# A recurrence with sparse attention on one core: scans over every second step, the causal mask inside the maximum, the decay mask on two engines, a first projection in fp32, and a new order

## The chip, the cores and the metric

The kernel runs on one core of a Trainium2 chip. The core has engines that run side by side, each with its own queue of instructions: TensorE (PE, matrix products; PEld is its weight load), VectorE (DVE), ScalarE (ACT), GpSimd (POOL) and SyncE (SP, which here only issues transfers). Semaphores order them. Matrix products write PSUM; everything else lies in SBUF. The metric is the device time of one execution in microseconds. A profile comes from one further execution.

## The reference

The inputs are r, k, v, w of shape (4 batches, 8 heads, 768 steps, 48), a bonus u per head, and the weights of a layer of four attention experts, of which two are taken per token.

```python
for t in range(S):                                   # recurrence
    cur = np.einsum('bhd,bhe->bhde', u[None] * kt, vt)
    y[:, :, t] = np.einsum('bhd,bhde->bhe', rt, state + cur)
    state = wt[:, :, :, None] * state + np.einsum('bhd,bhe->bhde', kt, vt)
...
x = y of all heads side by side                      # (4, 768, 384)
logits = x @ w_gate; topk = the 2 best of 4; w = softmax of their logits
for e in range(E):                                   # 4 experts, 64 wide
    q, k, v = x @ wq[e], x @ wk[e], x @ wv[e]
    scores = np.where(causal, -1000000000.0, scale * (q @ k.transpose(0, 2, 1)))
    a = softmax(scores)
    ye = a @ v @ wo[e]
    out += (w where e was taken) * ye
```

## The kernel before, in words

Work is cut into eight units: batch b, half g of the 768 steps. A unit's 384 steps are six chunks of 64 (C=64, NH=6). Its eight heads go as four pairs p, two heads on the 128 partitions.

The recurrence of a pair. SP loads lt (decay w, k and r, with the 48 features on partitions and steps along columns), nat (v, k, r with steps on partitions) and vy. Two scans on VectorE turn w into running products inside each chunk: `suf` (L407) backwards and `pre` (L411) forwards, each over 390 columns, six chunks of 65; `inv` (L409) is a reciprocal between them. Then k and r are scaled by them, kt (L414) and mr (L416, which overwrites pre). TensorE turns kt (ktp), ScalarE or VectorE brings it to SBUF (kts), ups (L462) is each chunk's contribution to the state, and five steps a pair on VectorE (L471) run the state wst along the chunks. ys (L481) scales the states. Within a chunk, aps (L526) is the 64x64 matrix between steps for two pairs at once; its upper part is kept by a multiplication with dec_mask, am (L535), on VectorE straight out of PSUM: one instruction of 128 partitions for the even pair, two of 64 partitions for the odd one, whose halves lie swapped. yps adds ys times pre (L504) and am times vy (L501) in PSUM. Separately uk (L421), ur (L424), rk (L427) and ux (L434 on ScalarE, six multiplications of 48 columns a pair, or L436 on GpSimd or VectorE) make the bonus term in xn, and addy (L510, one per head) adds yps to it.

The attention of a unit. xn is turned in three thirds of 128 features (xp, L248 or L252). Each is split into xh and xl (L557 ScalarE, L559 VectorE), two parts with fewer bits of mantissa; a product of fp32 accuracy is then three products: high by high, high by low, low by high. So run the projections to q and k (L601: three products to a third, three thirds, for two pairs of experts and for q and k: 36 in a unit) and to v and the gate's logits (L624). Scores (L689) are made for pairs of experts in blocks of 128 rows; four products L694 of a bf16 `causal` with a selection matrix `idh` add -1e9 above the diagonal. VectorE takes the negated maximum out of PSUM (L703), ScalarE the exponential with the row's sum (L705), TensorE turns the result (tp), ScalarE or VectorE copies it (ATa, ATb), and L747 multiplies it with v. Then come the gate's weights, gb (L793) and the output product op (L815).

At the start TensorE runs 94 filler products `warm` (L865) that nothing reads, wherever nothing else is ready.

The order. Every operation is recorded with the engines that may take it, a cost on each, its inputs and its outputs. `order()` then lists the operations engine by engine: each has a due time (its place in its unit's stretch plus a number from the table `WISH`, by kind and unit), and the planner takes the earliest due among those that could start by its own costs (t_dve, t_scan, t_act, t_exp, t_pool and the T_ numbers). It picks the engine where several may take an operation, keeps a `port` between VectorE and GpSimd for the kinds in `BOTH`, and reckons gaps where TensorE changes the shape of its tile. The program is emitted in that order, with a dependency added for the port. One queue of transfers, SP's, carries all loads and stores in the planned order.

Of the kernel before, what the change touches and what calls it, by code (L numbers as in the profile page):

```python
# [19 lines left out]
NP = H // 2  # L20
C = 64
# [5 lines left out]
WB = NH * (C + 1) + 1  # L27
# [7 lines left out]
def t_scan(cols):  # L35
    return 65 + 2.09 * cols
# [6 lines left out]
def t_exp(cols):  # L43
    return 237 + 0.834 * cols


def t_pool(cols):
    return 60 + 2.25 * cols


class Slot:
# [6 lines left out]
    def __call__(self):  # L58
# [14 lines left out]
BOTH = {"DVE": {"suf", "pre", "ys", "kt", "mr", "uk", "ur", "ux", "yl", "wsqk", "wsvg", "wso", "carry", "gate", "masks"},  # L73
        "POOL": {"kt", "mr", "uk", "ur", "ux", "gate", "g4"}}
# [12 lines left out]
class Plan:  # L87
# [8 lines left out]
    def add(self, kind, engs, fn, r=(), w=(), want=None, mode="F", alt=None, claim=()):  # L96

        o = dict(engs=engs, fn=fn, want=(self.now if want is None else want) + WISH[kind][self.unit],  # L100
                 n=len(self.ops), kind=kind, mode=mode, alt=alt, deps=set(), outs=[], slots=[], ready={})
# [21 lines left out]
    def order(self, free, slack=60.0, width=40):  # L123
# [11 lines left out]

        def push(o):
            for e in o["engs"]:
                insort(cand[e], (o["want"], o["n"]))
# [3 lines left out]

        for o in ops:
            if need[o["n"]] == 0:
                push(o)
        done = []
# [3 lines left out]
        while len(done) < len(ops):  # L150
# [52 lines left out]
            for s in o["slots"]:  # L203
                s.left -= 1
                s.ends[e] = max(s.ends.get(e, 0.0), end)
                if s.left == 0:
                    bufs[s.tag][s.idx] = s.ends
            for k in o["outs"]:
                x = ops[k]
                x["ready"][e] = max(x["ready"].get(e, 0.0), end)  # L210
                need[k] -= 1
                if need[k] == 0:
                    push(x)
            done.append(o)
# [5 lines left out]
def rwkv_moe(ctx: ExitStack, tc: tile.TileContext, wkr, vY, nat, uN,  # L220
# [52 lines left out]

    one_suf = cst.tile([128, WB], F32, name="one_suf")
    nc.gpsimd.memset(one_suf, 0.0)
    nc.gpsimd.memset(one_suf[:, 1:WB].rearrange("p (c j) -> p c j", j=C + 1)[:, :, C:C + 1], 1.0)  # L276
    inv_pre = cst.tile([128, NH, C + 1], F32, name="inv_pre")
# [30 lines left out]
    sel = cst.tile([128, 3 * E, HD], BF16, name="sel")  # L308
    tri = cst.tile([128, E, E], F32, name="tri")
# [3 lines left out]
    nc.gpsimd.memset(idh, 0.0)  # L313

    def masks(e):
        nc.scalar.copy(identb, ident)
        for a in range(2):
            for h in range(2):
                p = slice(64 * h, 64 * h + 64)
                nc.scalar.copy(idh[p, a, 64 * a:64 * a + 64], ident[p, 64 * h:64 * h + 64])  # L320

    def masks2(e):
        for a in range(2):
            for h in range(2):
                p = slice(64 * h, 64 * h + 64)
                nc.vector.tensor_scalar(causal[p, a, :], d128[p], 64.0 * (a - h), -1.0e9, op0=ALU.is_gt, op1=ALU.mult)
# [7 lines left out]
    def weights(n, src, cols, parts=1):  # L334
# [4 lines left out]
        wts[n] = (h, l)  # L339
# [11 lines left out]
    def rwkv(b, g, v0, v1):  # L351
# [9 lines left out]

        two = []
        for p in range(NP):
            n = f"{b}{g}{p}"
            want(p / (NP + 1))
            lt = sb([128, WB + 2 * NH * C], F32, "lt", f"lt{n}")
            if first and p == 0:
                load("ld", lambda lt=lt: lt()[:, 0:WB], wkr[b, g, p, :, 0:WB], WB, [(lt, 0)])
                load("ld", lambda lt=lt: lt()[:, WB:], wkr[b, g, p, :, WB:], 2 * NH * C, [(lt, 1)])
            else:  # L370
                load("ld", lt, wkr[b, g, p], WB + 2 * NH * C, [(lt, 0), (lt, 1)])
# [26 lines left out]
            pre = sb([128, NH, C + 1], F32, "pre", f"pre{n}")  # L398
            am = sb([128, NH, C], F32, "am", f"am{n}")

            def sfv(suf=suf):
                return suf()[:, 1:WB].rearrange("p (c j) -> p c j", j=C + 1)

            kt = sb([128, NH, C], F32, "kt", f"kt{n}")


            plan.add("suf", {"DVE": t_scan(WB)}, lambda e, suf=suf, w_=w_: nc.vector.tensor_tensor_scan(  # L407
                rev(suf()), rev(w_()), rev(one_suf), 0.0, op0=ALU.mult, op1=ALU.add), [(lt, 0)], [suf])
            plan.add("inv", {"DVE": 106}, lambda e, sfv=sfv: nc.vector.reciprocal(inv_pre[:, :, 0], sfv()[:, :, 0]),  # L409
                     [suf], ["inv_pre"])  # L410
            plan.add("pre", {"DVE": t_scan(WB)}, lambda e, pre=pre, w_=w_: nc.vector.tensor_tensor_scan(  # L411
                flat(pre()), w_()[:, 0:WB - 1], flat(inv_pre), 0.0, op0=ALU.mult, op1=ALU.add),
                [(lt, 0), "inv_pre"], [pre])
            plan.add("kt", prod(384), lambda e, k_=k_, sfv=sfv, kt=kt: E_[e].tensor_tensor(  # L414
                kt(), k_(), sfv()[:, :, 1:C + 1], op=ALU.mult), [(lt, 1), suf], [kt])
# [614 lines left out]
```

## Time and profile before

| what | value |
|---|---|
| three runs | 363.26, 363.70, 366.65 us, median 363.7 |
| the profiled execution | 363.1 us, its span 361.3 us |
| mean granted clock of TensorE | 0.985 of full speed |
| instructions in the span | 13097 |
| idle of GpSimd before kt, on suf | 35.0 us, 13 times |
| idle of ScalarE before the exponential, on the maximum | 34.3 us, 32 times |
| idle of TensorE's weight load before L504, on ys of GpSimd | 3.9 us, 4 times, longest 1.7 |
| loads by SP | 31 whole lt of 579.5 KB, 32 nat of 432.0 KB, 32 vy of 144.0 KB |

A group's row in the profile names the line, the engine, the operation, output<-input with their shapes and the count; behind the first bar stand the busy time of all and the mean of one in ns, behind the second the engine's idle time just before them and who ended it. Rows of a timeline are start, length, what ran, and in brackets the idle time before. The chain of work that ended last is followed back from the last instruction.

### The profile page before, as it was taken

How to read it: one execution, taken by the hardware profiler on the slowest of the kernel's cores; microseconds unless marked ns; L12 is line 12 of the kernel's file. 1: busy time of each engine (PE TensorE's matmuls, PEld its weight loads, DVE VectorE, ACT ScalarE, POOL GpSimd, SP SyncE). 2: the span in 40 equal slices, each digit the busy share in tenths (PEclk: the TensorE clock that was granted, in tenths of full speed). 3: DMA queues.
4: the chain of work that ended last, by engine and by line, in shares of the span. 5: the costliest groups of instructions: out<-in, count | busy, mean ns of one | idle time of the engine just before them, and what ended most of it. 6: DMA issues, size and time to landing. Idle time of an engine off the chain costs nothing.

```text
span 361.3 us, 13097 instructions
## 1 busy us (share of the span) xinstructions
PE 343.7 (95%) x5357; PEld 267.6 (74%) x5357; DVE 305.0 (84%) x797; ACT 203.2 (56%) x611; POOL 142.0 (39%) x263
## 2 busy tenths in 40 slices
PE   7999989899999999999999999999999999999986
PEld 3555777687876878787877868887787878868755
DVE  6899899779889999988989998998999983567462
ACT  3262354573757645864745646767674464556553
POOL 3466276545462143463853246435333210201010
PEclk9999999789999999999999999999999999999989
DMA  7995547135633634336245344645120000000101
GB/s 251 373 318 184 176 128 256 35 92 174 200 133 116 181 104 135 116 132 201 74 139 187 116 151 133 219 136 161 35 95 24 18 5 33 34 2 3 65 3 65
DMA packets 18060, 45.20 MB, mean 125 GB/s; under 512 B 2000, under 2 KB 9424, under 8 KB 18000
## 3 DMA queue, kind: packets, MB, share of 16 engines
q1 hardware_dynamic: 18000, 44.37, 37.1%
q8 instruction: 42, 0.69, 0.8%
q14 instruction: 18, 0.15, 0.1%
HBM read 39.64 MB, written 4.72 MB: 123 GB/s over the span
## 4 chain that ended last, share of the span: by engine, by line
PE 68%; DVE 16%; ACT 5%; DMA 3%; issue 3%; POOL 3%; SPq 0%; ACTq 0%; DVEq 0%; POOLq 0%
PE pp L601 12%; PE yp L747 9%; PE op L815 7%; PE sp L689 7%; PE tp L248 6%; PE vp L624 5%; ACT a L705 4%; PE tp L252 3%; DVE mx L703 3%; PE warm L865 3%; PE aps L526 3%; PE ups L462 3%; PE yps L504 3%; DVE am L535 2%; DVE wst L471 2%
## 5 line engine op out<-in xcount | busy, mean ns | idle before, releaser
L705 ACT ACTIVATE a<-sp,mx 128x128 f32<-128x128 f32 (+5 forms) x96 | 60.3, 634 | 39.4 <-DVE mx L703 34.3
L703 DVE TENSOR_REDUCE mx<-sp 128x1 f32<-128x128 f32 (+5 forms) x96 | 55.3, 616 | 7.8 <-PE sp L694 5.7
L414 POOL TENSOR_TENSOR kt<-lt,suf 128x384 f32<-128x384 f32 x28 | 26.8, 959 | 46.3 <-DVE suf L407 35.0
L471 DVE SCALAR_TENSOR_TENSOR wst<-wst,suf,ups 112x48 f32<-112x48 f32 x160 | 39.7, 258 | 2.4 <-ACT wst L256 0.2
L434 ACT ACTIVATE xn<-nat,rk 128x48 f32<-128x48 f32 x120 | 30.7, 331 | 15.7 <-DVE rk L427 15.5
L256 ACT COPY ATa<-tp 128x512 f32<-128x512 f32 (+3 forms) x72 | 34.1, 488 | 9.3 <-PE tp L248 6.0
L601 PE MATMUL pp<-xh,wh_qk 128*128 128x384 f32 x96 | 38.5, 401 | 0.0
L421 POOL TENSOR_TENSOR nat<-nat,u_sb 128x288 f32<-128x288 f32 x32 | 25.7, 803 | 31.8 <-DMA nat<-in_nat_dram 21.4
L747 PE MATMUL yp<-ATa,v_sb 128*64 128x384 f32 (+2 forms) x240 | 37.5, 441 | 0.0
L407 DVE TENSOR_TENSOR_SCAN suf<-lt,one_suf 128x390 f32<-128x390 f32 x32 | 31.3, 977 | 2.2 <-DMA lt<-in_wkr_dram 1.3
L248 PE MATMUL tp<-ident,a 128*128 128x128 f32 x191 | 30.2, 282 | 2.8 <-ACT a L705 1.4
L601 PE MATMUL pp<-xl,wh_qk 128*128 128x384 f32 x96 | 32.7, 341 | 0.0
L601 PE MATMUL pp<-xh,wl_qk 128*128 128x384 f32 x96 | 32.7, 340 | 0.0
L411 DVE TENSOR_TENSOR_SCAN pre<-lt,inv_pre 128x390 f32<-128x390 f32 x32 | 31.9, 995 | 0.1
L416 POOL TENSOR_TENSOR pre<-lt,pre 128x384 f32<-128x384 f32 x21 | 19.1, 913 | 28.2 <-DVE pre L411 21.4
L535 DVE TENSOR_TENSOR am<-aps,dec_mask 64x384 f32<-64x384 f32 (+1 forms) x48 | 26.6, 554 | 3.6 <-PE aps L526 2.8
L248 PEld LDWEIGHTS tp<-ident,a 128*128 128x128 f32 x191 | 22.2, 142 | 8.3 <-ACT a L705 4.9
L504 PE MATMUL yps<-ys,pre 64*64 64x48 f32 (+1 forms) x704 | 25.1, 222 | 2.1 <-POOL ys L481 2.0
L689 PE MATMUL sp<-Kh,Qh 64*128 64x384 f32 (+4 forms) x128 | 26.6, 396 | 0.4 <-DVE am L535 0.3
L865 PE MATMUL warm<-one_suf 128*128 128x512 bf16 x94 | 25.5, 410 | 1.4 <-POOL one_suf L276 1.4
L504 PEld LDWEIGHTS yps<-ys,pre 64*64 64x64 f32 (+1 forms) x704 | 21.3, 134 | 7.3 <-POOL ys L481 3.9
L501 PE MATMUL yps<-vy,am 64*64 64x48 f32 x768 | 25.9, 219 | 0.2 <-issue 0.2
(134 smaller groups left out, 876.9 us busy)
## 6 DMA issues: line engine op xcount, KB each, us to landing
lt<-in_wkr_dram SPq DMA_DIRECT2D x31, 579.5 KB, 4.7
nat<-in_nat_dram SPq DMA_DIRECT2D x32, 432.0 KB, 4.1
vy<-in_vY_dram SPq DMA_DIRECT2D x32, 144.0 KB, 2.7
out_dram<-ob SPq DMA_DIRECT2D x24, 192.0 KB, 1.9
w_qk<-in_wqk_dram SPq DMA_DIRECT2D x1, 768.0 KB, 7.8
w_vg<-in_wvg_dram SPq DMA_DIRECT2D x1, 390.0 KB, 7.3
lt<-in_wkr_dram SPq DMA_DIRECT2D x1, 384.0 KB, 5.0
w_o<-in_wo_dram SPq DMA_DIRECT2D x1, 384.0 KB, 4.0
```

The lines of the kernel that those rows point to most:

```text
L248: nc.tensor.transpose(o()[:, i * 128:i * 128 + 128], src, ident)
L256: nc.scalar.copy(o, i)
L411: plan.add("pre", {"DVE": t_scan(WB)}, lambda e, pre=pre, w_=w_: nc.vector.tensor_tensor_scan(flat(pre()), w_()[:, 0:WB - 1], flat(inv_pre ...
L471: nc.vector.scalar_tensor_tensor(new, ws[0:112, c0 + c - 1, :], sfv()[0:112, c, 0:1], u()[0:112, o], op0=ALU.mult, op1=ALU.add)
L504: nc.tensor.matmul(yps[h]()[half(q), o], pre()[r, c, 0:C], ys()[r, c, :], start=i == 0, stop=False)
L535: nc.vector.tensor_tensor(am()[o], aps()[i, 0:NH * C].rearrange("p (c j) -> p c j", j=C), dec_mask[i, None, :].to_broadcast([i.stop - i.st ...
L601: nc.tensor.matmul(pp()[:, 0:384], w[:, qk, k, cs], x()[:, k, :], start=(k == j == 0), stop=(k == j == 2))
L689: nc.tensor.matmul(spv(x)[:, h, :], q()[p, t], flat(k())[p, o], start=j == 0, stop=j == 2 and h < np_ - 1)
L703: plan.add("max", {"DVE": t_dve(n)}, lambda e, x=x, mx=mx: nc.vector.tensor_reduce(mx(), spv(x), axis=AX.XY, op=ALU.max, negate=True), [sp ...
L705: plan.add("exp", {"ACT": t_exp(n)}, lambda e, x=x, y=y, mx=mx, a=a: nc.scalar.activation(a()[:, 0:n].rearrange("p (a n) -> p a n", a=np_) ...
L747: nc.tensor.matmul(yp()[e * 64:e * 64 + 64, lo:hi], v_sb[ep]()[:, j, e * 64:e * 64 + 64], at, start=(j == 0), stop=(j == nj - 1))
L865: plan.add("warm", {"PE": 216}, lambda e: nc.tensor.matmul(w()[:, 0:512], wz[:, 0:128], wz, start=True, stop=True), [], [w], want=1e6 if i ...
```

## The change

Six things are changed, and every number of the order with them.

1. Scans over every second step. The host lays out w, k and r with even and odd steps apart. w2 (L428) is the product of two neighbouring steps' decays; the scans suf (L430) and pre (L434) run over w2, 198 columns each. k of the even steps is multiplied by the odd step's decay (kw, L437) and r of the odd steps by the even step's (rw, L439), both in place, 192 columns each. kt (L441) and mr (L443) take 384 columns as before, with the scan's value used for two neighbouring steps and an output in which the two are interleaved again. lt grows from 1159 to 1166 columns.
2. The causal mask inside the maximum. The products L694 and idh are gone. `causal` is one row of zeros with a triangle of -1e9 at its end, in SBUF; a `tensor_tensor_reduce` on VectorE (L752) adds it to the scores, negates, writes the result to SBUF (tile a) and takes the minimum. It compiles to two instructions, the second of which brings out the accumulated minimum. The exponential (L757) then works in place on a, with scale -1.
3. The decay mask. An am is either masked on VectorE out of PSUM (L558, as before), or copied by ScalarE (L564) and then masked in place by GpSimd (L558 on POOL); the planner chooses, and where VectorE took it the second operation is dropped (`skip`).
4. One ux and one addy per pair instead of one per head.
5. The first unit's x is not split: xh stays fp32, there is no xl, and its projections (L639, L670) are plain fp32 products with the unsplit weights, each third by itself as soon as it is there.
6. The planner: costs of exponential, GpSimd and scores, a table ONLY that fixes an engine for some kinds and units, a new WISH table. The order of loads at the start is different too: two vy loads stand ahead of the first lt.

```diff
@@ order: an operation that was taken over is skipped
+            if o["skip"] is not None and o["skip"]["e"] == "DVE":
+                o["e"], o["t"], o["end"] = None, 0.0, 0.0
+                finish(o, o["ready"])
+                return
@@ scans
-            plan.add("suf", {"DVE": t_scan(WB)}, lambda e, suf=suf, w_=w_: nc.vector.tensor_tensor_scan(
-                rev(suf()), rev(w_()), rev(one_suf), 0.0, op0=ALU.mult, op1=ALU.add), [(lt, 0)], [suf])
+            plan.add("w2", prod(WB), lambda e, w2=w2, w_=w_: E_[e].tensor_tensor(w2(), w_(0), w_(1), op=ALU.mult),
+                     [(lt, 0)], [w2])
+            plan.add("suf", {"DVE": t_scan(WB)}, lambda e, suf=suf, w2=w2: nc.vector.tensor_tensor_scan(
+                rev(suf()), rev(w2()), rev(one_suf), 0.0, op0=ALU.mult, op1=ALU.add), [w2], [suf])
...
+            plan.add("kw", prod(192), lambda e, k_=k_, wv=wv: E_[e].tensor_tensor(
+                k_()[:, 0], k_()[:, 0], wv(1), op=ALU.mult), [(lt, 0), (lt, 1)], [(lt, 2)])
...
+            plan.add("kt", spread(384), lambda e, k_=k_, sfv=sfv, kt=kt: E_[e].tensor_tensor(
+                mixed(kt), k_(), both(sfv()[:, :, 1:]), op=ALU.mult), [(lt, 1), (lt, 2), suf], [kt])
@@ decay mask
-                    plan.add("am", {"DVE": 575 if x == 0 else 565}, mask, [(apk, x)], [(am, h)])
+                def masked(e, src, dst, o=slice(0, 128)):
+                    E_[e].tensor_tensor(dst, src, dec_mask[o, None, :].to_broadcast([o.stop - o.start, NH, C]), op=ALU.mult)
+
+                def evict(e, x=x, am=am, aps=apss[x]):
+                    for o, i in ((half(0), half(1)), (half(1), half(0))) if x else ((slice(0, 128),) * 2,):
+                        src = aps()[i, 0:NH * C]
+                        if e == "ACT":
+                            nc.scalar.copy(flat(am()[o]), src)
+                        else:
+                            masked(e, src.rearrange("p (c j) -> p c j", j=C), am()[o], o)
+                o = plan.add("am", {"ACT": 495 if x == 0 else 880, "DVE": 470 if x == 0 else 1090}, evict, [(apk, x), "dmask"], [am])
+                plan.add("msk", {"POOL": t_pool(384)}, lambda e, am=am: masked(e, am(), am()), [am], [am], skip=o)
@@ first projection
+                if first:
+                    wf = wts["qk"][2]
+
+                    def mm(e, k=k):
+                        nc.tensor.matmul(pp()[:, 0:384], wf()[:, (qk * 3 + k) * 256:(qk * 3 + k) * 256 + 256][:, cs], xh()[:, k, :],
+                                         start=k == 0, stop=k == 2)
+                    plan.add("proj", {"PE": 645}, mm, [(xh, k), wf] + ([pk] if k else []), [pk], claim=(K if qk else Q)[ep])
+                    continue
@@ scores, maximum and exponential
-                for a in range(2):
-                    for x in range(2):
-                        p = slice(64 * x, 64 * x + 64)
-                        nc.tensor.matmul(spv(x)[:, np_ - 1, w - 128:w], idh[p, a, :], causal[p, a, :], start=False, stop=a == 1)
...
-                plan.add("max", {"DVE": t_dve(n)}, lambda e, x=x, mx=mx: nc.vector.tensor_reduce(
-                    mx(), spv(x), axis=AX.XY, op=ALU.max, negate=True), [sp], [mx])
+                def lowest(e, x=x, mx=mx, a=a):
+                    nc.vector.tensor_tensor_reduce(
+                        out=a()[:, 0:n].rearrange("p (a n) -> p a n", a=np_), in0=spv(x),
+                        in1=causal[:, S - n:S].rearrange("p (a n) -> p a n", a=np_), scale=-1.0, scalar=3.0e38,
+                        op0=ALU.add, op1=ALU.min, accum_out=mx())
+                plan.add("max", {"DVE": t_dve(n) + T_TTR}, lowest, [sp, "masks"], [mx, a])
...
-                    a()[:, 0:n].rearrange("p (a n) -> p a n", a=np_), spv(x), AF.Exp, bias=mx(),
-                    accum_out=asum()[:, i, y:y + 1]), [sp, mx], [a, (asum, i, y)])
+                    a()[:, 0:n], a()[:, 0:n], AF.Exp, bias=mx(), scale=-1.0,
+                    accum_out=asum()[:, i, y:y + 1]), [mx, a], [a, (asum, i, y)])
@@ numbers of the order (one row of each table)
+ONLY = dict(
+    am="00000100",
...
-    addy=[-237.86, -225.24, -20.82, -95.05, -242.81, -38.73, -115.81, -23.26],
+    addy=[-144.26, -153.99, 0.61, 39.08, 79.54, 3.02, -136.24, -149.46],
...
-T_SC = (492, 561, 733, 902, 1084, 1261)
+T_SC = (385, 454, 626, 795, 977, 1154)
+T_TTR = 12
```

What the order does, in three places. A name is a tile and the numbers behind it unit and pair (suf001: batch 0, half 0, pair 1), then a running number. First VectorE at the start, before:

```order
L407 SCALAR_TENSOR_TENSOR suf000_131<-lt000_108,one_suf_66 128x390
L409 RECIPROCAL inv_pre_69<-suf000_131 128x6
L411 SCALAR_TENSOR_TENSOR pre000_147<-lt000_108,inv_pre_69 128x390
L407 SCALAR_TENSOR_TENSOR suf001_156<-lt001_116,one_suf_66 128x390
L416 TENSOR_TENSOR pre000_147<-lt000_108,pre000_147 128x6x64
L409 RECIPROCAL inv_pre_69<-suf001_156 128x6
L414 TENSOR_TENSOR kt001_174<-lt001_116,suf001_156 128x384
```

and now:

```order
L430 SCALAR_TENSOR_TENSOR suf000_132<-w2000_127,one_suf_68 128x198
L437 TENSOR_TENSOR lt000_110<-lt000_110 128x192
L439 TENSOR_TENSOR lt000_110<-lt000_110 128x192
L432 RECIPROCAL inv_pre_71<-suf000_132 128x6
L441 TENSOR_TENSOR kt000_145<-lt000_110,suf000_132 128x2x192
L434 SCALAR_TENSOR_TENSOR p2000_149<-w2000_127,inv_pre_71 128x198
L443 TENSOR_TENSOR pre000_156<-lt000_110,p2000_149 128x2x192
L428 TENSOR_TENSOR w2001_164<-lt001_120 128x199
```

The first pair's kt, which GpSimd took before, is now VectorE's, while GpSimd makes its w2.

Second TensorE where unit 0's projection begins, before (the rows ahead are fillers):

```order
L865 MATMUL warm_126<-one_suf_66 128x512
L601 MATMUL pp0000_676<-xh00_431,wh_qk_101 128x384
L601 MATMUL pp0000_676<-xh00_431,wl_qk_102 128x384
L601 MATMUL pp0000_676<-xl00_442,wh_qk_101 128x384
L601 MATMUL pp0000_676<-xh00_431,wh_qk_101 128x384
```

and now, at the last third:

```order
L918 MATMUL warm_122<-causal_66 128x512
L261 MATMUL xp002_662<-ident_77,xn00_265 128x128 x3
L639 MATMUL pp00_466<-xh00_455,w_qk_253 128x384 x4
L261 MATMUL ktp010_692<-ident_77,kt010_647 128x128 x3
L639 MATMUL pp0010_478<-xh00_455,w_qk_253 128x384 x2
```

Four of the twelve products stand earlier, among the fillers behind xp000, and two more a few rows on.

Third the masks and maxima of VectorE in unit 1, before:

```order
L535 TENSOR_TENSOR am010_891<-aps010_854,dec_mask_86 128x384
L535 TENSOR_TENSOR am011_899<-aps010_854,dec_mask_86 64x384 x2
L409 RECIPROCAL inv_pre_69<-suf013_879 128x6
L703 TENSOR_REDUCE mx0011_932<-sp00010_739 128x1
L510 TENSOR_TENSOR xn01_594<-yps010_901,xn01_594 128x3x48 x2
```

and now:

```order
L558 TENSOR_TENSOR am011_808<-aps010_774,dec_mask_95 64x384 x2
L682 COPY lg00_818<-vp000_767 128x4
L499 SCALAR_TENSOR_TENSOR wst1_83<-wst1_83,suf011_681,ups011_751 112x48 x3
L752 ISA a0000_835,mx0000_836<-sp00000_820,causal_66 128x128
L752 ISA mx0000_836 128x1
```

Only the odd pair's am is still there; each maximum has become two rows, the first with a second output.

More of the change, by code (lines that the diff above doesn't have):

```diff
@@ L94, in __init__, with add @@
         self.unit = 0
-    def add(self, kind, engs, fn, r=(), w=(), want=None, mode="F", alt=None, claim=()):
+    def add(self, kind, engs, fn, r=(), w=(), want=None, mode="F", alt=None, claim=(), skip=None):
+        only = ONLY.get(kind, "0" * 8)[self.unit]
+        if only != "0" and len(engs) > 1:
+            engs = {e: t for e, t in engs.items() if (e == "DVE") == (only == "2")}
         o = dict(engs=engs, fn=fn, want=(self.now if want is None else want) + WISH[kind][self.unit],
-                 n=len(self.ops), kind=kind, mode=mode, alt=alt, deps=set(), outs=[], slots=[], ready={})
+                 n=len(self.ops), kind=kind, mode=mode, alt=alt, deps=set(), outs=[], slots=[], ready={}, skip=skip)
         for k in r:
@@ L202, in order @@
             o["t"], o["e"], o["end"] = t, e, end
[L203 to L214, printed above, removed]
+            finish(o, {e: end})
         self.span = max(o["end"] for o in ops)
@@ L311, in rwkv_moe, with masks3 @@
                    allow_small_or_imprecise_dtypes=True)
[L313 removed]
     def masks(e):
         nc.scalar.copy(identb, ident)
[L317 to L320 removed]
+    def masks3(e):
+        nc.vector.tensor_scalar(dec_mask[0:64], d128[0:64, 0:C], 0.0, None, op0=ALU.is_gt)
+        nc.vector.tensor_scalar(dec_mask[64:128], d128[64:128, 0:C], -64.0, None, op0=ALU.is_gt)
     def masks2(e):
[L323 to L326, printed above, removed]
+        nc.vector.tensor_scalar(causal[:, S - 128:S], d128, 0.0, -1.0e9, op0=ALU.is_gt, op1=ALU.mult)
         nc.vector.tensor_scalar(onehot, dcol, drow, None, op0=ALU.is_equal)
@@ L542, in rwkv @@
         want(NP / (NP + 1))
-        xh = sb([128, 3, 384], F32R, "xh", f"xh{b}{g}")
-        xl = sb([128, 3, 384], F32R, "xl", f"xl{b}{g}")
-        allx = [(xn, p, h) for p in range(NP) for h in range(2)]
+        xh = sb([128, 3, 384], F32 if first else F32R, "xh", f"xh{b}{g}")
+        xl = xh if first else sb([128, 3, 384], F32R, "xl", f"xl{b}{g}")
         need = {0: [0, 1], 1: [1, 2], 2: [2, 3]}
@@ L620, in vproj, with mm @@
                 step(0.333)
+                if first:
+                    wf = wts["vg"][2]
+                    def mm(e, k=k):
+                        nc.tensor.matmul(vp()[:, 0:260], xh()[:, k, o], wf()[:, k * 260:k * 260 + 260], start=k == 0, stop=k == 2)
+                    plan.add("vproj", {"PE": 440}, mm, [(xh, kk) for kk in range(3)] + [wf] + ([vp] if k else []), [vp], claim=v_sb)
+                    continue
                 def mm(e, k=k):
```

319 lines of the change are left out of this document (186 added, 133 removed).

## The prediction

> **What bounds the kernel now.** I read the busy times first, then the same by stretch, then the chain of work that ended last, then the groups.
>
> ```profile
> span 361.3 us, 13097 instructions
> PE 343.7 (95%) x5357; PEld 267.6 (74%) x5357; DVE 305.0 (84%) x797; ACT 203.2 (56%) x611; POOL 142.0 (39%) x263
> 0.00:39.30 39.30, 35.07 (x506) 18.49 (x507) 33.16 (x86) 15.06 (x43) 19.97 (x35) 1.00 0.80 284
> 39.30:280.00 240.70, 232.82 (x3875) 188.25 (x3874) 221.45 (x578) 145.09 (x449) 112.26 (x189) 0.99 0.42 133
> 280.00:361.30 81.30, 75.83 (x980) 60.88 (x978) 50.38 (x135) 43.07 (x121) 9.73 (x39) 0.98 0.07 25
> PE 68%; DVE 16%; ACT 5%; DMA 3%; issue 3%; POOL 3%; SPq 0%; ACTq 0%; DVEq 0%; POOLq 0%
> ```
>
> A window's row gives its ends and length, the busy time of PE, PEld, DVE, ACT and POOL, then clock, DMA share and GB/s. The cuts are mine: 39.3 us is the start of unit 0's projection, and at 280 us the scans are over. Up to 39.3 PE mostly runs fillers and the loads and VectorE set the pace. From 39.3 to 280 TensorE is 97% busy (232.8 of 240.7) and VectorE 92% (221.5): two engines at the limit, and the chain is PE's with DVE pieces in it. After 280 PE is 93% busy and VectorE 62%. So a microsecond taken from VectorE alone in the middle stage is worth less than a microsecond, and the same holds for TensorE.
>
> **VectorE, part by part.**
>
> ```profile
> L411 DVE TENSOR_TENSOR_SCAN pre<-lt,inv_pre 128x390 f32<-128x390 f32 x32 | 31.9, 995 | 0.1
> L407 DVE TENSOR_TENSOR_SCAN suf<-lt,one_suf 128x390 f32<-128x390 f32 x32 | 31.3, 977 | 2.2 <-DMA lt<-in_wkr_dram 1.3 <-POOL ys L481 0.9
> L535 DVE TENSOR_TENSOR am<-aps,dec_mask 64x384 f32<-64x384 f32 x32 | 17.8, 555 | 0.7
> L510 DVE TENSOR_TENSOR xn<-yps,xn 128x144 f32<-128x144 f32 x64 | 16.4, 297 | 2.4 <-PE yps L501 2.1
> L613 DVE TENSOR_TENSOR Kl<-pp,Kh 128x384 fp32r<-128x384 f32 x16 | 8.8, 550 | 1.7 <-ACT Kh L612 1.6
> L703 DVE TENSOR_REDUCE mx<-sp 128x1 f32<-128x384 f32 x16 | 8.3, 551 | 2.9 <-PE sp L694 1.9 <-ACT a L705 0.8
> L630 DVE COPY lg<-vp 128x4 f32<-128x4 f32 x24 | 3.7, 154 | 2.2 <-ACT v_sb L256 1.9 <-PE vp L624 0.2
> 9.37 0.53 DVE L416 TENSOR_TENSOR pre<-lt,pre 128x384 f32<-128x384 f32 x1
> 9.82 0.18 DVE L409 RECIPROCAL inv_pre<-suf 128x6 f32<-128x6 f32 x1
> 9.92 0.51 DVE L414 TENSOR_TENSOR kt<-lt,suf 128x384 f32<-128x384 f32 x1
> ```
>
> (The last three rows are a timeline: start, length.) A row counts about 0.08 us that the next one overlaps: the 0.53 at 9.37 is followed at 9.82, the 0.18 at 9.82 at 9.92. I count a row less 0.08. Between 144 columns (297 ns) and 384 (550) one column costs 1.05 ns and the rest 0.145 us, which is 0.065 after the overlap. A scan of 390 columns at 0.98 us then costs 2.1 ns a column, and one of 198 about 0.56: 0.42 less. Then:
> - 64 scans: -26 us (64 x 0.42, rounded down). That half the columns do not give half the time by more than the fixed 0.145 is my assumption. Ends -24 and -27.
> - New products: w2 on VectorE 18 times at 199 columns, kw and rw 33 times at 192, each 0.27: +13.8.
> - Decay masks: 48 become 29, 19 x 0.47: -8.9. They move to ScalarE and GpSimd (below).
> - Additions L510: 64 of 144 columns become 32 of 288: -64 x 0.22 + 32 x 0.37 = -2.2.
> - Work that changes engine in the new order: kt and mr +10 at 0.47, uk and the in-place r product +13 at 0.37, kts +7 at 0.47; ys -5, ux -6, ob -4, xl -3, v_sb -4 and small ones. Together +12.8 - 9 = +3.8, at the same price by columns.
> - The maxima. A masked maximum reads the scores from PSUM and the mask from SBUF, adds, writes 128 to 768 columns and reduces. No row shows that. The nearest: a reduction of 384 columns from PSUM takes 551 ns and a two-input subtraction of 384 columns with one input in PSUM 550, so one column a beat for either. I take no change. Upper end: 2.1 ns a column as the scan has, since both combine two operations (rival 4). Lower end: the same.
> - The second instruction of each maximum, which brings out the accumulated value: 96 of them. Nearest row: the 128x4 copy, 154 ns, less 0.08 = 0.07: +6.7. Ends 0 and 200 ns less 0.08 (ScalarE's accumulator read, quoted below), +11.5.
>
> Sum on VectorE: -26 + 13.8 - 8.9 - 2.2 + 3.8 + 6.7 = -12.8, ends -20 and -6. In the middle stage it is about -10: seven of eight units' scans and masks, and 70 of the 96 readings.
>
> [...]
>
> **TensorE.**
>
> ```profile
> 39.30:280.00 240.70, 10.58 (x140) 4.39 (x140) 0.99 0.42 133
> 280.00:361.30 81.30, 3.85 (x52) 1.62 (x52) 0.98 0.07 25
> 296.05 0.29 PE L694 MATMUL sp<-causal,idh 64*128 64x128 bf16 x4
> 296.17 0.35 PE L252 MATMUL xp<-ident,xn 64*128 64x64 f32 x6
> 39.34 3.14 PE pp L601 x18
> 190.34 1.51 PE L747 MATMUL yp<-ATa,v_sb 128*64 128x384 f32 x8
> 191.68 0.82 PE L747 MATMUL yp<-ATb,v_sb 128*64 128x256 f32 x8
> ```
>
> The first two rows are the windows of L694 alone: 140 and 52 mask products, four to a block of scores. Their rows overlap, so a block costs from its start to the next work's: 0.12 us (296.05 to 296.17). 35 blocks in the middle stage: -4.2; 13 after: -1.6. Unit 0's projection: 18 products in 3.14 us (a row of the chain) is 0.52 for the three that make a third. The fp32 product that takes their place: eight 64-column records in 1.34 us (190.34 to 191.68) are two pairs, 0.67 a pair that fills 128 columns, so 12 x (0.67 - 0.52) = +1.8; if a pair's halves ran one after another, a third would be 0.34 and the change -2.2. Four of the twelve now run before xp002 in place of fillers: -4 x 0.67 = -2.7. The nine of v: +0.5 by the same ratio. Middle stage: -4.2 + 1.8 - 2.7 + 0.5 = -4.6. The fillers keep their count (94) and take only idle time.
>
> **ScalarE and GpSimd.**
>
> ```profile
> L705 ACT ACTIVATE a<-sp,mx 128x128 f32<-128x128 f32 (+5 forms) x96 | 60.3, 634 | 39.4 <-DVE mx L703 34.3 <-PE ktp L252 1.6 <-DVE inv_pre L409 1.6
> L705 ACT ACTIVATION_READ_ACCUMULATOR a<-sp,mx 128x1 f32 x96 | 19.2, 200 | 0.0
> L434 ACT ACTIVATE xn<-nat,rk 128x48 f32<-128x48 f32 x120 | 30.7, 331 | 15.7 <-DVE rk L427 15.5
> L414 POOL TENSOR_TENSOR kt<-lt,suf 128x384 f32<-128x384 f32 x28 | 26.8, 959 | 46.3 <-DVE suf L407 35.0 <-DVE pre L411 3.4 <-DVE wl_vg L345 2.9
> L803 ACT CAST yh<-yr 128x384 fp32r<-128x384 f32 x14 | 7.1, 518 | 7.6 <-DVE yr L801 7.6
> L612 ACT CAST Kh<-pp 128x384 fp32r<-128x384 f32 x16 | 7.7, 483 | 3.1 <-PE pp L601 2.7
> ```
>
> The exponentials read SBUF instead of PSUM: a cast of 384 columns takes 518 ns from SBUF and 483 from PSUM, 96 x 0.035 = +3.4. 19 mask copies at 0.4 (483 less 0.08): +7.6. 30 more L434 multiplications at 0.25: +7.5. ScalarE is 60% busy in the middle stage and waits 34.3 us for maxima, so I cost this at nothing; what hides it is that waiting. GpSimd loses about a third of kt (959 ns a piece), uk and ur and gains 13 kw, 18 rw, 14 w2 (0.5 each by columns) and 17 masks (0.96): about +22 to 164, 45% of the span; in the middle stage 112 becomes about 130 of 240. It stays off the bound by itself; as a step in chains it is rival 1.
>
> Behind ScalarE's new mask copies wait exponentials and score evictions, and behind GpSimd's masks the next pair's products; the second product L501 waits for the mask.
>
> **The start.**
>
> ```profile
> 5.71 0.97 DVE L407 TENSOR_TENSOR_SCAN suf<-lt,one_suf 128x390 f32<-128x390 f32 x1 [1.29 <-DMA lt<-in_wkr_dram]
> 7.01 1.57 DVE L411 TENSOR_TENSOR_SCAN pre<-lt,inv_pre 128x390 f32<-128x390 f32 x1
> 6.81 0.95 POOL L414 TENSOR_TENSOR kt<-lt,suf 128x384 f32<-128x384 f32 x1 [4.12 <-DVE suf L407]
> 1.17 2.38 SPq L265 DMA_DIRECT2D lt<-in_wkr_dram  x5
> ```
>
> SP issues five loads in 2.38 us, 0.48 each; the new order puts two vy loads ahead of the first lt: +1.0 before the first scan, and w2 on GpSimd another 0.7. Against it the shorter scans and no xl (-0.6). The rows of VectorE up to unit 0's last addition count 87 instead of 83, about +1.3 us by columns. PE has 31 fewer fillers to run through, so the first projection can come when its thirds are ready. I take 0 (ends -2 and +3).
>
> **The half clock.**
>
> ```profile
> 60.00:80.00 20.00, 17.97 (x241) 14.48 (x241) 15.80 (x45) 12.54 (x45) 10.95 (x18) 0.83 0.28 88
> 64.33 2.25 POOL ys L481
> 66.63 0.33 PE L504 MATMUL yps<-ys,pre 64*64 64x48 f32 x8 [1.51 <-POOL ys L481]
> ```
>
> Here TensorE waits 1.5 us for a ys on GpSimd, and the granted clock in these 20 us is 0.83: 3.4 us of clock are lost. A new order has other waits. Ends 0 and -4.9 (wait and clock gone); I take -2, since the shorter scans let ys be made earlier but GpSimd is fuller.
>
> **The sum.** Start 0. Middle stage: -4.6 if TensorE alone set it, about -10/0.92 = -11 if VectorE alone did; I take -7.5, between them, because both are over 90%. Half clock -2. Last stage: -1.6 for masks, and up to +1.3 where a maximum and its reading stand on the path (0.11 a block): -0.8. Together -10.3: span 351.0. The execution profiled was 363.1 beside its span of 361.3, +1.8, and the median of the runs, 363.7, is 0.6 above it: 353.4, said as 353.5.
>
> **Rivals.**
> 1. The decay mask becomes the wait (slower). The mask was one DVE row of 0.55 us; on 17 occasions it is now a copy (0.48), a hand-over and a GpSimd product (0.96 by the kt row), about 1.2 us later, on two engines whose queues hold other work. If each held L501 and PE found nothing else, +20 us in place of -10: span +10, 373. It decides when half of the 17 are exposed. For it: the scan at 7.01 took 1.57 instead of 0.97 while GpSimd ran kt at 6.81, so the two engines block each other, and GpSimd's work grows by 22 us. Against: a mask may wait behind other units' matmuls, as PE has a second unit's attention to run. Chance 0.13. [...]
> 2. TensorE holds and the start slips: -4.6 - 0.8, +2.7 at the start, no gain in the half clock: about 361 for a run, within 1%. For it: the 97%. Chance 0.20.
> 3. VectorE was what held PE: -11 and the whole half-clock gain, -5, -1: 347. For it: 92% busy with PE fed by it. Chance 0.12.
> 4. The masked maximum runs at the scan's 2.1 ns a column. 448 columns on average x 1.05 x 96 = +45 on VectorE: near 395. Against: the 551 beside 550. Chance 0.03.
>
> **How the numbers follow.** The forecast itself, 349 to 358, has 0.5; with 0.02 for what I have not thought of. Within 1% is 360.0 to 367.3, about what a measurement of this kernel can tell from no change. Faster: 0.5 + 0.12 + a quarter of rival 2 and 0.01 = 0.68. Same: the rest of rival 2 and partly exposed masks, 0.18. Slower: rivals 1 and 4 less those, 0.14. The range reaches to rival 3 and to rival 2: 345 to 362.
>
> **What would show it.** Scan rows near 0.56 us and DVE busy near 292; two rows to each maximum, the first at about 0.55 for 384 columns; GpSimd near 164; no mask products on PE; PEclk full in the slices at 60 to 80 us; unit 0's projection at 38 to 42 us; PE's waits for ys and am. It would be wrong if PE's idle before L501 or L504 grows by several us, if DVE's time falls by less than 6, or if PE's busy time falls without the span.

## The result and the profile after

The changed kernel takes 353.64 us (median of four runs, 351.11 to 354.13) against 364.64 for the kernel before beside it (363.26 to 366.65): ratio 0.968, 95% interval 0.961 to 0.975. A second set gave 353.58 against 362.9, 0.973 (0.966 to 0.981). The profiled execution took 351.11 us with a span of 349.2. The forecast, 353.5, hit the median; the sum behind it, 351.0 for the span, was 1.8 us too high for this execution and 3 too low for that of the second set (354.0). Some executions of a kernel lie more than 1.5% above its fastest; the ratios leave these out, the medians don't.

The page of the changed kernel, as far as it answers to the lines shown of before:

```profile
span 349.2 us, 12872 instructions
PE 331.4 (95%) x5139; PEld 257.3 (74%) x5148; DVE 294.9 (84%) x909; ACT 217.9 (62%) x648; POOL 158.5 (45%) x294
PE 60%; DVE 23%; DMA 5%; ACT 4%; issue 3%; POOL 3%; SPq 0%; ACTq 0%; POOLq 0%; DVEq 0%
```

TensorE's busy time fell by 12.3 us and the span by 12.1: its idle time is what it was. Not all of the 12.3 us are instructions: the granted clock was 0.985 in the profile of before and is 0.999 here, which over 361.3 us is about 5 us of slower work (an estimate). VectorE's fell by 10.1, ScalarE's rose by 14.7 and GpSimd's by 16.5. Now the same by stretch. The borders are drawn anew: in this order the projection of unit 0's last third starts at 40.45 us, and the scans are over at 289 instead of 280.

```profile
0.00:40.60 40.60, 34.75 (x477) 18.37 (x486) 32.19 (x93) 14.86 (x43) 16.22 (x32) 1.00 0.76 265
40.60:289.00 248.40, 240.18 (x3965) 192.02 (x3968) 229.92 (x717) 165.79 (x503) 133.19 (x229) 1.00 0.41 131
289.00:349.20 60.20, 56.43 (x713) 46.88 (x704) 32.76 (x103) 37.26 (x103) 9.14 (x34) 0.99 0.10 34
```

The middle stretch is 7.7 us longer and the last one 21 us shorter: the new order does more attention while the scans still run. So the terms by stage can't be checked one against one, only their sum. In the middle TensorE is 97% and VectorE 93% busy, as before.

The groups that the change touched:

```profile
L434 DVE TENSOR_TENSOR_SCAN p<-w,inv_pre 128x198 f32<-128x198 f32 x32 | 21.4, 668 | 0.2
L430 DVE TENSOR_TENSOR_SCAN suf<-w,one_suf 128x198 f32<-128x198 f32 x32 | 19.4, 619 | 4.3 <-POOL w L428 2.4 <-POOL ys L509 1.9
L428 DVE TENSOR_TENSOR w<-lt 128x199 f32<-128x199 f32 x18 | 7.0, 394 | 0.0
L437 DVE TENSOR_TENSOR lt<-lt 128x192 f32<-128x192 f32 x19 | 7.0, 374 | 1.6 <-DMA lt<-in_wkr_dram 1.6
L439 DVE TENSOR_TENSOR lt<-lt 128x192 f32<-128x192 f32 x14 | 4.9, 350 | 0.6 <-DMA lt<-in_wkr_dram 0.6
L752 DVE CUSTOM_DVE_ANT_0 a<-sp,causal 128x384 f32<-128x384 f32 x16 | 8.5, 547 | 0.2 <-PE sp L741 0.2
L752 DVE DVE_READ_ACCUMULATOR2_ANT mx<- 128x1 f32 x96 | 7.9, 83 | 0.0
L757 ACT ACTIVATE a<-a,mx 128x128 f32<-128x128 f32 (+5 forms) x96 | 63.9, 667 | 19.6 <-DVE mx L752 18.0
L558 POOL TENSOR_TENSOR am<-am,dec_mask 128x384 f32<-128x384 f32 x17 | 17.1, 1005 | 9.5 <-ACT am L564 7.1 <-DVE Kl L658 1.0 <-DVE suf L430 0.8
```

The scans' mean is 619 and 668 ns. The masked maximum of 384 columns takes 547 ns where the reduction took 551. Its second instruction has a row of 83 ns. A timeline shows what that costs:

```profile
111.26 0.68 DVE L752 CUSTOM_DVE_ANT_0 a<-sp,causal 128x512 f32<-128x512 f32 x1
111.86 0.08 DVE L752 DVE_READ_ACCUMULATOR2_ANT mx<- 128x1 f32 x1
111.86 0.69 DVE L752 CUSTOM_DVE_ANT_0 a<-sp,causal 128x512 f32<-128x512 f32 x1
```

The next instruction starts in the same moment as the reading: it costs the queue nothing. So it is after 84 of the 96 readings; behind most of the others VectorE waits for another engine.

### The profile page after: what moved, and what is told of

Its sections match the earlier page's. It is cut to its first block, busy times and chain, and to the rows that moved or that the text cites. A ratio compares the mean times of both kernels' runs of the same rounds, so it can differ in the third digit from the quotient of the medians.

```text
span 349.2 us, 12872 instructions
## 1 busy us (share of the span) xinstructions
PE 331.4 (95%) x5139; PEld 257.3 (74%) x5148; DVE 294.9 (84%) x909; ACT 217.9 (62%) x648; POOL 158.5 (45%) x294
## 4 chain that ended last, share of the span: by engine, by line
PE 60%; DVE 23%; DMA 5%; ACT 4%; issue 3%; POOL 3%; SPq 0%; ACTq 0%; POOLq 0%; DVEq 0%
PE pp L646 10%; PE sp L741 8%; PE yp L799 7%; PE op L867 6%; PE vp L676 6%; PE tp L261 5%; DVE wst L499 3%; DVE am L558 3%; PE tp L265 3%; DMA lt<-in_wkr_dram 3%; DMA nat<-in_nat_dram 3%; DVE a L752 2%; PE yps L532 2%; PE ups L490 2%; PE aps L553 2%
## 5 line engine op out<-in xcount | busy, mean ns | idle before, releaser
L757 ACT ACTIVATE a<-a,mx 128x128 f32<-128x128 f32 (+5 forms) x96 | 63.9, 667 | 19.6 <-DVE mx L752 18.0
L752 DVE CUSTOM_DVE_ANT_0 a<-sp,causal 128x128 f32<-128x128 f32 (+5 forms) x96 | 56.6, 617 | 8.3 <-PE sp L741 7.7
L461 ACT ACTIVATE xn<-nat,rk 128x48 f32<-128x48 f32 x150 | 36.5, 324 | 14.1 <-DVE rk L454 13.9
L646 PE MATMUL pp<-xh,wh_qk 128*128 128x384 f32 x84 | 32.2, 383 | 0.0
L443 POOL TENSOR_TENSOR pre<-lt,p 128x384 f32<-128x384 f32 x20 | 18.7, 937 | 21.2 <-DVE p L434 15.4
L918 PE MATMUL warm<-causal 128*128 128x512 bf16 x85 | 23.9, 418 | 2.4 <-POOL causal L288 1.4
L509 POOL TENSOR_TENSOR ys<-wst,suf 112x288 f32<-112x288 f32 (+1 forms) x25 | 17.8, 714 | 15.4 <-DVE wst L499 13.0
L441 POOL TENSOR_TENSOR kt<-lt,suf 128x384 f32<-128x384 f32 x19 | 17.7, 937 | 15.2 <-DVE suf L430 7.7
L799 PEld LDWEIGHTS yp<-ATa,v_sb 128*64 128x64 f32 x240 | 15.3, 136 | 12.5 <-issue 9.1
L430 DVE TENSOR_TENSOR_SCAN suf<-w,one_suf 128x198 f32<-128x198 f32 x32 | 19.4, 619 | 4.3 <-POOL w L428 2.4
```

Of the source, the lines that this page charges most:

```text
L461: nc.scalar.mul(xn()[:, i, (2 * p + h) * D:(2 * p + h + 1) * D], vn()[:, i, h * D:(h + 1) * D], rk()[:, i, h:h + 1])
L646: nc.tensor.matmul(pp()[:, 0:384], w[:, qk, k, cs], x()[:, k, :], start=(k == j == 0), stop=(k == j == 2))
L752: nc.vector.tensor_tensor_reduce(out=a()[:, 0:n].rearrange("p (a n) -> p a n", a=np_), in0=spv(x), in1=causal[:, S - n:S].rearrange("p (a ...
L757: plan.add("exp", {"ACT": t_exp(n)}, lambda e, x=x, y=y, mx=mx, a=a: nc.scalar.activation(a()[:, 0:n], a()[:, 0:n], AF.Exp, bias=mx(), sca ...
L799: nc.tensor.matmul(yp()[e * 64:e * 64 + 64, lo:hi], v_sb[ep]()[:, j, e * 64:e * 64 + 64], at, start=(j == 0), stop=(j == nj - 1))
L918: plan.add("warm", {"PE": 216}, lambda e: nc.tensor.matmul(w()[:, 0:512], wz[:, 0:128], wz, start=True, stop=True), [], [w], want=1e6 if i ...
```

## The experiments

All kernels below keep the order of the kernel that they start from, unless it says otherwise: only what is emitted in a place is altered, not what the planner is told. Medians are given with the ratio to the kernel before in the same set and its 95% interval. Where a time is given as + or -, a run of the changed kernel is compared with 353.58, the median of the run that comes first here, and a run of the kernel before with the median of that kernel in its own set.

**The changed kernel again.** No edit.

> The changed kernel itself once more, as the base for the runs beside it: 351 to 354 us, ratio to the kernel before 0.965 to 0.972, granted clock over 0.99.

353.58 us, ratio 0.973 (0.966 to 0.981). Missed in part: the ratio lies just above what was expected, one of the four runs, the profiled one, took 355.77 us, and two of the four had a granted clock of 0.988 and 0.990. More on the clock below.

**The causal products' time given back to TensorE.**

```diff
...
+                for a in range(2):
+                    for x in range(2):
+                        p = slice(64 * x, 64 * x + 64)
+                        nc.tensor.matmul(spv(x)[:, np_ - 1, w - 128:w], causal[p, 0:128], causal[p, 0:128], start=False, stop=a == 1)
```

> The changed kernel with four bf16 products of zeros added to each block of scores, in the place where the causal products stood; the order is otherwise the same. Theory A (TensorE sets the pace from 40 us on): 48 blocks x 0.12 us = +5.8 us over the changed kernel, 359 us. Theory B (VectorE sets it, TensorE has slack): under +2 us, 355 us or less. Both halves bound: about +3.5.

358.68 us, +5.1; ratio 0.985 (0.976 to 0.993). The two profiles at full clock (1.000 here, 0.999 in the first of the changed kernel) differ by 353.4 - 349.2 = 4.2 us. Theory A's 5.8 came out at 70 to 90%.

**VectorE's saving given back.**

```diff
+            def more(w2=w2):
+                nc.vector.tensor_tensor_scan(junk, w2()[:, 0:MORE], one_suf[:, 0:MORE], 0.0, op0=ALU.mult, op1=ALU.add)
...
+            def scan1(e, suf=suf, w2=w2, more=more):
+                more()
...
+MORE = 46
```

> The changed kernel with a scan of 46 columns into an unread tile ahead of each of the 64 scans, 0.16 us each, +10 us on VectorE, which is all that VectorE's busy time had fallen (305.0 to 294.9); the order is the same. Theory A (TensorE): under +3 us, under 356.5. Theory B (VectorE): +8 to +11 us, 362 to 364.

357.6 us, +4.0; ratio 0.981 (0.972 to 0.989). VectorE's busy time rose by 12.5 us (307.4), more than the 10 that were meant. So neither theory: some third of VectorE's time shows. The intervals of this run and of the one above overlap that of the changed kernel, so each alone is worth less than the pair that follows.

**Both given back.**

> The changed kernel with both costs given back at once: four products of zeros to each block of scores (+5.1 us alone) and the 46-column scan ahead of each scan (+4.0 alone). If the two engines hold the time one after another, in different places: +9, 362 to 364, which is the time before, and the parts explain the whole gain in this order. If they hide one another: +5 to +6, 359, and some 4 us of the gain are the order's own.

361.67 us against 363.26 for the kernel before, ratio 0.995 (0.992 to 0.998): 2.2 to 2.7 of the 2.7 to 3.2% are gone. At the same clock all of it is: the four runs at a granted clock of 0.994 or 0.995 that the ratio counts have a median of 362.5 us, where the kernel before has 361.5 at that clock (below). The profile at full clock:

```profile
span 358.0 us, 13327 instructions
PE 339.8 (95%) x5340; PEld 261.7 (73%) x5340; DVE 305.9 (85%) x973; ACT 218.3 (61%) x648; POOL 157.6 (44%) x294
```

The span is 358.0 against 349.2, +8.8, with both engines' busy times close to those of before (343.7 and 305.0). The costs add up (4.2 or 5.1, and 4.0), as they would if the two engines held the time in different places, one after the other. It isn't ruled out that part of this is only the disturbance of a fitted order, which knows nothing of the work that was put in. So these costs are rather upper bounds of what the parts are worth.

**The decay masks back on VectorE.**

```diff
-                        if e == "ACT":
-                            nc.scalar.copy(flat(am()[o]), src)
-                        else:
+                        if True:
                             masked(e, src.rearrange("p (c j) -> p c j", j=C), am()[o], o)
...
-                plan.add("msk", {"POOL": t_pool(384)}, lambda e, am=am: masked(e, am(), am()), [am], [am], skip=o)
+                plan.add("msk", {"POOL": t_pool(384)}, lambda e: None, [am], [am], skip=o)
...
+        if o["kind"] == "am":
+            o["e"] = o["how"] = "DVE"
...
+        if o["kind"] == "msk":
+            continue
```

> The changed kernel with all decay masks on VectorE straight out of PSUM, at the place of ScalarE's copies, without the 17 products on GpSimd; nothing else moves. VectorE +9 us, ScalarE -8, GpSimd -16. Theory A (TensorE): within 2 us of the changed kernel. Theory B (VectorE): +5 to +9 us. If the way over ScalarE and GpSimd had been what TensorE waits for: -2 us or more.

357.39 us, +3.8; ratio 0.983 (0.976 to 0.990), between theories A and B, part of it clock (0.986 to 0.993 in its four runs). VectorE's busy time rose by 8.3 us to 303.2. The way over ScalarE and GpSimd is not what holds the kernel: without it the kernel is slower, not faster, and in the changed kernel's profile TensorE's products waited for a mask of GpSimd once, for 0.2 us, and its weight loads twice, for 0.6 us in all.

**The same savings in the order of before.** First without the causal products:

```diff
-                for a in range(2):
-                    for x in range(2):
-                        p = slice(64 * x, 64 * x + 64)
-                        nc.tensor.matmul(spv(x)[:, np_ - 1, w - 128:w], idh[p, a, :], causal[p, a, :], start=False, stop=a == 1)
```

> The kernel before without the 192 causal products (the causal mask is left out of the result), in the same order. Theory A (TensorE sets the pace): 48 x 0.12 = -5.8 us, 358 to 359 us. Theory B (VectorE): under -2 us.

363.81 us against 362.74, ratio 1.003 (1.000 to 1.007): nothing, outside theory A's range, where giving the same products back to the changed kernel cost 4 to 5 us. The middle stretch of this kernel:

```profile
39.30:280.00 240.70, 227.69 (x3727) 182.72 (x3726) 220.34 (x576) 144.58 (x448) 112.39 (x189) 0.99 0.43 133
```

TensorE's busy time there fell from 232.8 to 227.7 us, and in the same time the other engines got through as much as before (576 instructions on VectorE instead of 578, 448 on ScalarE instead of 449, 189 on GpSimd in both): the five microseconds are idle now. Some 1 to 2 of them are clock and not products (an estimate): at a granted clock of 0.83 at 60 to 80 us the kernel before lost 3.4 us, and this profile lost 1.2 to 2.3 in the stretch, by the 0.99 in the row above and the 0.994 over its span of 359.7 us. One place, in the timelines of TensorE, VectorE and GpSimd; the first two rows are of the kernel before, the others of this one:

```profile
104.47 0.40 PE L252 MATMUL xp<-ident,xn 64*128 64x64 f32 x6 [0.82 <-DVE xn L510]
103.44 0.45 DVE L427 TENSOR_REDUCE rk<-nat 128x6 f32<-128x288 f32 x1 [0.85 <-POOL nat L424]
103.86 0.40 PE L252 MATMUL xp<-ident,xn 64*128 64x64 f32 x6 [1.84 <-DVE xn L510]
102.84 0.45 DVE L427 TENSOR_REDUCE rk<-nat 128x6 f32<-128x288 f32 x1 [2.00 <-POOL nat L424]
103.21 0.51 DVE L510 TENSOR_TENSOR xn<-yps,xn 128x144 f32<-128x144 f32 x2
99.62 0.80 POOL L421 TENSOR_TENSOR nat<-nat,u_sb 128x288 f32<-128x288 f32 x1 [1.44 <-DMA nat<-in_nat_dram]
101.26 0.79 POOL L421 TENSOR_TENSOR nat<-nat,u_sb 128x288 f32<-128x288 f32 x1 [0.84 <-PE yps L504]
```

TensorE comes to xp earlier and waits 1.84 us (0.82 before) for L510, which stands in VectorE's queue behind an rk that waits 2.00 us (0.85 before) for a product of GpSimd; GpSimd had itself stood waiting shortly before, for a load (1.44 us) and for a yps of TensorE (0.84 us). Neither TensorE nor VectorE was short of time here: the next thing in the queue wasn't ready.

**Then with additions in place of the scans, and with both.**

```diff
-            ... nc.vector.tensor_tensor_scan(rev(suf()), rev(w_()), rev(one_suf), 0.0, op0=ALU.mult, op1=ALU.add)
+            ... nc.vector.tensor_tensor(suf(), w_(), one_suf, op=ALU.add)
...
-            ... nc.vector.tensor_tensor_scan(flat(pre()), w_()[:, 0:WB - 1], flat(inv_pre), 0.0, op0=ALU.mult, op1=ALU.add)
+            ... nc.vector.tensor_tensor(flat(pre()), w_()[:, 0:WB - 1], flat(inv_pre), op=ALU.add)
```

> The kernel before with each of the 64 scans of 390 columns replaced by one addition of 390 columns (the recurrence's products of decays are left out of the result), in the same order: 0.40 us less each, -26 us on VectorE. Theory A (TensorE): -3 us or less. Theory B (VectorE): -15 us or more. Both bound together: -5 to -9.

358.94 us, ratio 0.990 (0.984 to 0.995): -3.8 us for 23 us less on VectorE (busy 281.6 instead of 305.0), between theory A's -3 and the -5 to -9 of both bound together. Part of it is clock: the two runs at 0.994 or 0.995 have a median of 358.9 against 361.5 for the kernel before at that clock.

> The two together: no causal products and additions in place of the scans (both left out of the result), in the order of before. Theory A: about -6 to -9 us, 355 to 358. Theory B: -15 to -18. If each had only hidden the other, more than the sum of the two alone.

360.9 us, ratio 0.993 (0.988 to 0.997), by the medians no better than the additions alone; no range that was expected was met. Nine of its ten runs had a granted clock of 0.976 to 0.986; the one at 0.995 took 357.12. Theory B is out, and in this order what was taken off TensorE (5.8 us as counted) and VectorE (23) is worth 3 to 4 us together at the same clock: the five runs at 0.985 or 0.986 have a median of 360.4 against 363.4, the one at 0.995 has 357.1 against 361.5.

**A new order from the old due times.**

```diff
-T_SC = (492, 561, 733, 902, 1084, 1261)
+T_SC = (385, 454, 626, 795, 977, 1154)
...
-            plan.add("suf", {"DVE": t_scan(WB)}, ...
+            plan.add("suf", {"DVE": t_dve(WB)}, ...
```

(and the same for pre; otherwise as with both)

> The kernel before without the causal products and with additions in place of the scans (both left out of the result), as in the run with both, but with these costs told to the planner, which makes a new order by the old due times. If the old order is what kept the saving (in-order queues that wait for what was planned there): 350 to 356 us. If due times have to be fitted anew to the costs: 358 or more, as without replanning (360.9).

372.92 us, ratio 1.028 (1.023 to 1.032): 12 us slower than the same work in the old order. The second expectation had the direction, but named 360.9 for it.

```profile
span 370.9 us, 12759 instructions
PE 340.0 (92%) x5191; PEld 262.1 (71%) x5191; DVE 292.5 (79%) x819; ACT 201.0 (54%) x596; POOL 124.3 (33%) x252
```

Every engine has less to do than in the kernel before, and TensorE's share fell from 95% to 92%. Here an order worked out from due times that belong to other costs is worse than a stale one.

**The half clock.** Fillers in the wait that had come before it:

```diff
+                    for _ in range(FILL.get(n, 0)):
+                        nc.tensor.matmul(yps[1](), wz[:, 0:128], wz, start=True, stop=True)
...
+FILL = {"013": 7}
```

> The kernel before with seven filler products of 512 columns ahead of the yps of unit 1's last pair, where TensorE had waited 1.5 us for ys. If the wait was what brought the half clock of 6.8 us behind it: granted clock up from 0.985 to about 0.995 and -3 us, 361 to 362 us. If not: clock still 0.985, time within 1 us of before.

361.1 us, ratio 0.995 (0.993 to 0.998), clock 0.994 to 1.000 in all ten runs. The window of 60 to 80 us, which in the kernel before had a granted clock of 0.83, with 0.50 from 67.6 to 74.4 us:

```profile
60.00:80.00 20.00, 19.00 (x324) 14.22 (x325) 18.32 (x51) 13.29 (x48) 10.57 (x22) 1.00 0.35 107
```

The half clock is gone from there (1.00), and it was worth 1.6 us, half of what was expected. The clock also sorts the runs of the kernel before: over all sets, 19 runs at 0.985 or 0.986 have a median of 363.4 us, 15 at 0.994 or 0.995 one of 361.5. The changed kernel's four runs at 0.994 or 0.995 have 353.6: at the same clock the change is worth 7.9 us.

**The start.**

```diff
+    early = [o for o in todo if o["kind"] == "ldv"][:2]
+    todo = [o for o in todo if o not in early]
+    at = [i for i, o in enumerate(todo) if o["kind"] == "ld"][1] + 1
+    todo[at:at] = early
```

> The changed kernel with the first two vy loads behind the first pair's two lt loads instead of ahead of them; nothing else moves. The first scan starts 0.9 us earlier (5.7 instead of 6.6). If the start is on the path to the end: -0.5 to -1 us. If loads or later work hold it (lt and nat of pairs 2 and 3 come when they came): within 0.5 us.

351.66 us, ratio 0.971 (0.967 to 0.974). That is 1.9 us under the changed kernel's median, but its ratio lies inside the intervals of that (0.968 and 0.973), and the spans at nearly the same clock are 349.8 (0.998) and 349.2 (0.999). What was to be tried didn't happen: the first scan started at 6.57 us, not at 5.7. The issue of the first lt and the start of w2 on GpSimd, first in the changed kernel, then here:

```profile
2.10 0.91 SPq L278 DMA_DIRECT2D lt<-in_wkr_dram  x2
5.99 0.61 POOL L428 TENSOR_TENSOR w<-lt 128x199 f32<-128x199 f32 x1 [3.14 <-DMA lt<-in_wkr_dram]
1.16 0.89 SPq L278 DMA_DIRECT2D lt<-in_wkr_dram  x2
5.92 0.61 POOL L428 TENSOR_TENSOR w<-lt 128x199 f32<-128x199 f32 x1 [3.08 <-DMA lt<-in_wkr_dram]
```

The loads were issued 0.94 us earlier, and the w2 that waits for them began 0.07 us earlier. So whether the start is on the path stays open, and so does what the 1.9 us are.

With fillers as well:

```diff
+                    for _ in range(4 if n == "013" else 0):
+                        nc.tensor.matmul(yps[1](), wz[:, 0:128], wz, start=True, stop=True)
...
+                for _ in range(5 if n == "000" else 0):
+                    nc.tensor.matmul(ktp()[:, 512:1024], wz[:, 0:128], wz, start=True, stop=True)
```

> The same, and filler products where TensorE waits and a half clock has followed in some profiles of the changed kernel: five ahead of the first turned kt, four ahead of the yps of unit 1's last pair. If the half clock follows such waits: clock 0.995 to 1.0, and 1 to 2 us less than the changed kernel, 351 to 352. If not: as the run with the loads alone.

352.86 us, ratio 0.973 (0.970 to 0.976), clock 0.993 in two of four runs. Missed: it is no faster than with the loads alone, and the granted clock of the profiled run was 0.993 where 0.995 to 1.0 was expected. The five fillers ahead of the first kt ran where they were meant to (0.46 us of that wait is left), but those ahead of the yps did not run in the wait:

```profile
64.35 1.04 PE L522 MATMUL yps<-causal 128*128 128x512 bf16 x4 [0.91 <-DVE am L562]
```

They stood 0.91 us themselves, where the yps had waited 1.00 us in the changed kernel's profile, so this run says nothing on that wait.

## Why the prediction was right

*The total.* The sum was -10.3. Measured are -11.0 and -9.3 in the two sets, of which 7.9 at the same clock. That the forecast met the median to 0.2 us is luck: the middle term was a choice between -4.6 and -11, errors in VectorE's terms cancelled, and the runs of the changed kernel alone spread from 351.1 to 355.8 us.

*VectorE, -12.8.* Its busy time fell by 10.1. Several sizes inside were off. The scans saved 22.4 us (31.9 + 31.3 - 21.4 - 19.4), not 26: where nothing ran on GpSimd they take 0.57 us, and 0.56 was worked out, but the mean is 0.62 and 0.67. The readings cost nothing instead of 6.7. The products w2, kw and rw cost 18.9 us of rows, 14.8 less the overlap, against 13.8. The work that changed engine cost about 8 us instead of 3.8 (its rows, each less 0.08): the new order also gave VectorE eight more ATa copies (32 instead of 24), which the prediction's list doesn't name, and an in-place product of r took 546 ns instead of 487. The masked maximum runs at the reduction's pace, as taken (547 and 551 ns).

*TensorE, -4.6 and -1.6.* The causal products are worth 4.2 to 5.1 us where 5.8 were counted. The fp32 product's price, 0.67 us a third, held: three of them, six records, took 2.20 us at 25.41, or 0.73 with the start of the row. That term and unit 0's early thirds were not tried alone. TensorE's busy time fell by more than the sum has, 12.3 us, but some 5 of these are the clock.

*The middle stage, -7.5, "between them, because both are over 90%".* The size held, and so did the reading that neither engine alone sets the time: giving back TensorE's share costs 4 to 5 us, VectorE's 4, both 8 to 9. But the sum speaks as if these savings came with the instructions, and that failed. In the order of before, the causal products are worth nothing, the scans 3.8 (2.5 at the same clock) and both 3 to 4, of 7.9 at the same clock, though they take more off VectorE than the change did. And the new order alone is worth nothing: with both costs given back it takes 362.5 us where the kernel before takes 361.5. So less work and the order fitted to it are worth more together than the two apart. How much of the rest the other parts have (the fp32 projection, the decay mask on two engines, one ux and one addy a pair) the runs do not separate. That new costs alone do not make a good order is shown: with the old due times the time was 12 us worse than in the old order. The prediction put a price on every part and none on the new order. The place at 103.86 us above shows one way in which that comes: work that is done sooner only waits longer for the next thing in an unchanged queue.

*The start, 0.* The first scan started at 6.63 instead of 5.71 us, and the last third's projection 1.1 us later (40.45 instead of 39.34). Inside the ends given (-2 and +3). Of the 1.7 us that the prediction put ahead of the first scan, the product w2 came as counted (0.64 us from its start to the scan's), but not the 1.0 for the loads: w2 could start 0.28 us after the time at which the scan had started before, and issuing the lt loads first again brought 0.07.

*The half clock, -2.* The size held, the mechanism in part. In the kernel before, filling the wait for ys took the half clock away (1.00 instead of 0.83 at 60 to 80 us), for 1.6 us, and the changed kernel's runs have a higher clock (0.988 to 1.000) than those of before (0.976 to 0.995). But the wait in that place didn't go, it became one of 1.00 us for am, and a full clock isn't certain in the changed kernel either: its second profile has a granted clock of 0.990, where the first has 0.999.

*The last stage, -0.8.* It can't be separated, since the new order moved work out of it.

*The rivals.* The decay mask as a wait (373 us) fell: the 17 products on GpSimd took 1005 ns each, TensorE waited less than 1 us for them in all, and with the masks back on VectorE the kernel was slower by 3.8. TensorE alone (361) fell, as adding to VectorE cost 4 us; VectorE alone (347) fell, as adding to TensorE cost 4 to 5; both rest on the pair, since each interval alone overlaps that of the changed kernel. The slow masked maximum (395) fell by its row.

## What to carry to other kernels

In this kernel, where two engines are both over 90% busy in a fitted order, taking work away showed little until the order was fitted again, while adding it showed at once. So bracket what a part is worth: taking it out of the old kernel with the order left alone is likely to give too little, giving its cost back to the finished kernel too much (both argued here, not shown), and in between it counts only together with the order. Before reading a test, look in its trace whether the thing that was to move has moved: the start and one of the fillers above hadn't. And sort runs by granted clock before reading a difference of half a per cent.

## What the runs showed of the hardware

- Reading out an accumulated minimum is a row of 83 ns, and the next instruction starts in the same moment (111.86 and 111.86 us), so here after 84 of 96: nothing to pay.
- The scans of 198 columns took 0.57 us where nothing ran on GpSimd, 0.62 and 0.67 on average, and up to 1.16 beside a GpSimd instruction (71.48 us, beside an L443 of GpSimd). It went the other way too: at 94.71 us a w2 on GpSimd took 0.98 us beside a scan of 0.56, where the median of its 14 rows is 0.62. The ys on GpSimd that TensorE waited for in the kernel before took 2.29 us, beside a product (64.28 us) and a scan (65.14 us) on VectorE; the two others of its width in unit 1 took 1.21 and 1.34. No run here took VectorE's rows away to see that ys alone.
- In the kernel before the granted clock was 0.50 from 67.6 to 74.4 us and from 347.4 to 350.8 us, stretches of 6.8 and 3.4 us. They began 2.4 and 2.5 us after TensorE had begun a wait of 1.5 and one of 1.3 us (at 65.1 and 344.9 us). Not every such wait had one behind it: in the changed kernel's first profile a wait of 1.25 us at 109.7 was followed by none. Filling the wait of 1.5 us took the half clock away in that one place. What decides whether a wait brings a half clock, and how long that lasts, no run shows.
